# Where the value products of attention are issued: next to a round's scores, and a pair's second set one round earlier

## The chip, the cores and the metric

The kernel runs on one core of a Trainium2 chip. The metric is the device time of one execution in microseconds (us). PE is the matrix engine TensorE, PEld its weight loads, DVE is VectorE, ACT is ScalarE, POOL is GpSimd, and SP is the engine that issues the DMAs. Each engine executes the instructions of its own queue in the order in which the program issues them; between engines they wait for each other by semaphores.

## What is computed

Block-causal attention over 4 batches, 8 heads, 576 positions and head size 64; its output feeds a mixture of 8 experts (2304 tokens, width 512, hidden 1024) whose gate weights are normalised alternately over rows and columns eight times; that feeds a last two-layer network with a squared ReLU.

```python
scores = scale * np.matmul(q, k.transpose(0, 1, 3, 2))
mask = block_i >= block_j                      # blocks of 64 positions
attn = softmax(np.where(mask, scores, -1e9))
x = np.matmul(attn, v)                         # -> (2304, 512)
P = sinkhorn(exp(x @ w_gate), 8 rounds)        # (2304, 8)
for e in range(8):
    out += P[:, e:e + 1] * (np.maximum(x @ w1[e], 0) @ w2[e])
r = np.maximum(out @ w_in, 0); result = (r * r) @ w_out
```

## The kernel before

The 32 heads are worked off as 16 pairs (`PAIRS`). A pair has `R = 6` rounds of scores: the nine key-block widths are packed into six groups (`ROUNDS`), and `scores` issues the groups of an even round and of the next odd one together, so that only even rounds have scores. The whole attention is one software pipeline over rounds `r`, counted through all pairs: in round `r` the pair `r // 6` has its scores, and later steps of earlier rounds follow at fixed distances. Steps of round group i of a pair:

- scores on PE (`scores`, L563), into PSUM tiles sc and, in the pair's round 4, a small rest tile sct;
- one round later the maxima on DVE (`soft`, L582 to L593) and the exponentials on ACT (`expo`, L604);
- `LAG = 3` rounds after the scores the normalisation of pb by DVE (L620) or POOL (L616);
- four rounds after the scores the transposes on PE (`trans`, L643; the last group has a fifth, L646), five rounds after them their copies out of PSUM on ACT (`evac`, L657 and, for the fifth, L659), into ptx for the groups 0 to 2 and into pty for 3 to 5;
- the value products on PE (`pv`, L687), in two sets: the first reads ptx, the second pty. `PVT` holds the round, counted from the pair's start, in which each set is issued: 8 and 11;
- one round after a set (`PVD = 1`) ACT's copy of it into xs (`pv_copy`, L694), and after the second set the DMAs of xs to memory (`xout`, L699) and the pair's part of the gate logits (`logits_part`, lp on PE, L713, and its addition into prob on DVE, L724 or L726), the latter for pairs 4 and up.

Inside a round the steps are issued in the order of the table `ORDER`; "soft" is the maxima and normalisation, "pvc" the copy of a set with its DMAs, "load" the loads and `logits_part`, "hi" the `evac` copies, "exp" the exponentials, "S" the scores, "fill" the filling, "pv" the sets, "T" the transposes. The events of one engine therefore stand in its queue in this order, round after round.

The filling is the work of the experts. It is cut into pieces (a product m of a stage, L309 to L311, or an output tile y, L371 to L373), each costed at about one microsecond, and `fill` issues as many per round as the budget of 1.05 us allows. A product is followed by DVE's combination (L315), by ACT's ReLU where a hidden block is complete (L284), and by conversions of the next stage's weights (ACT L169 and L177, POOL L170, L178 and L153). Filling can only begin when the first third of the tokens has its gate logits (`logits`, lg on PE, L820) and its operands formed (`form`: sums f on POOL, L237; copies x on ACT, L243; rests x on DVE or POOL, L244). These two run as a task that is queued behind the DMAs of pair 7 (`first_ready`), two steps per round after a head start of three steps. So pairs 0 to 8 have no filling in their rounds, and the later ones have. In the attention part the products, outputs, transposes, sets, sct and lp share four PSUM buffers. After the attention the rest of the filling runs without it, to the end of the program.

```python
PVT = (8, 11)
PVD = 1
...
def turn(r):
    return [(n, z) for z, o in enumerate(PVT) for n in [(r - o) // R]
            if (r - o) % R == 0 and 0 <= n < PAIRS]
...
for r in range(total + R + LAG):
    for e in ORDER:
        events[e](r)
```

Of the kernel before, what the change touches and what calls it, by code (L numbers as in the profile page):

```python
# [55 lines left out]

POFF = {7: 0, 3: 2496, 6: 512, 5: 2752, 8: 1024, 0: 1600, 2: 1728, 4: 1984, 1: 2368}

ORDER = ["soft", "pvc", "load", "hi", "exp", "S", "fill", "pv", "T"]

POOL_NORM = (1, 4, 6, 8)

# [1 line left out]

LAG = 3

PVT = (8, 11)

PVD = 1

# [29 lines left out]
def fused_kernel(ctx: ExitStack, tc: tile.TileContext, q, k, v, wg, w1, w2, u1, u2, ident, out):  # L100
# [401 lines left out]
    def attention():  # L502
        with ExitStack() as es:
# [267 lines left out]
# [3 lines that stand above are left out]
# [35 lines left out]
# [3 lines that stand above are left out]
# [130 lines left out]
```

## Time and profile before

| what | before |
|---|---|
| median of 3 runs | 2097.63 us (2095.95 to 2098.12) |
| span of the profiled execution, first to last instruction | 2094.2 us |
| PE busy | 2064.7 us (99%) |
| DVE busy | 1653.6 us (79%) |
| POOL busy | 1566.2 us (75%) |
| ACT busy | 922.2 us (44%) |
| mean granted TensorE clock | 0.997 of full speed |

The profiled execution is one execution recorded by the hardware profiler; its device time without the recording isn't given beside it, so its span is set against the runs: the median lies 3.4 us above the span. A matmul counts as busy from its start to a modelled end, and neighbours overlap, so the busy share of PE isn't how near it is to its peak; the chain of waits and the starts of instructions say more. In a row of the chain, the time of a piece is the time that the chain spent in it. In a row of a timeline, the bracket at the end says how long the engine was idle before the instruction and what released it. The shape behind a matmul's names begins with the part of the array that it uses (contraction rows by output rows): 64\*64 for scores, 128\*64 for the sets, 128\*128 for transposes and filling.

### The profile page before, as it was taken

What the parts mean: (1) busy time and instruction counts of PE and PEld (TensorE: products, weight loads), DVE (VectorE), ACT (ScalarE), POOL (GpSimd) and SP (SyncE); (2) the same over time, 40 slices, a digit from 0 to 9 for tenths busy, and PEclk for the clock granted to TensorE, in tenths of its full rate; (3) what the DMA queues carried; (4) which work ended last, traced back from release to release, by engine and by line L of the source; (5) the groups of instructions that cost most, each with busy time, mean ns of one, the idle gap of its engine ahead of it and who ended that gap; (6) DMA issues with size and microseconds to landing.
All of it is one profiled execution on the core that took longest, in us unless ns stands there. A gap on an engine that the chain in (4) does not pass through costs nothing.

```text
span 2094.2 us, 34229 instructions
## 1 busy us (share of the span) xinstructions
PE 2064.7 (99%) x11603; PEld 1828.2 (87%) x11603; DVE 1653.6 (79%) x2906; ACT 922.2 (44%) x2299; POOL 1566.2 (75%) x1767
## 2 busy tenths in 40 slices
PE   8989999999999999999999999999999999999999
PEld 5767888999999899999999989999999989989898
DVE  7777678878878677878888768778787668989987
ACT  7876443334433533334434343333434344444442
POOL 4374566788887677778898777777897767989974
PEclk9999999999999999999999999999999999999999
DMA  5524111322222322232322233233222123231311
GB/s 177 153 89 130 52 64 68 117 90 93 94 79 94 120 77 87 100 106 86 101 78 91 94 106 98 89 106 109 78 76 86 61 81 103 69 131 61 103 69 51
DMA packets 80718, 194.71 MB, mean 93 GB/s; under 512 B 26144, under 2 KB 27296, under 8 KB 80544
## 3 DMA queue, kind: packets, MB, share of 16 engines
q1 hardware_dynamic: 80544, 192.53, 27.7%
q8 instruction: 92, 1.51, 0.3%
q14 instruction: 82, 0.67, 0.1%
HBM read 169.95 MB, written 20.97 MB: 91 GB/s over the span
## 4 chain that ended last, share of the span: by engine, by line
PE 90%; DVE 7%; ACT 1%; issue 1%; POOL 1%; DMA 0%; SPq 0%; ACTq 0%; DVEq 0%; POOLq 0%
PE y L371 15%; PE y L372 15%; PE y L373 15%; PE m L309 13%; PE m L311 13%; PE m L310 13%; PE T L643 2%; PE pv L687 2%; PE sc L563 2%; DVE c L289 2%; DVE acc L384 1%; DVE c L315 1%; DVE h L291 1%; DVE h L285 1%; ACT h L290 1%
## 5 line engine op out<-in xcount | busy, mean ns | idle before, releaser
L371 PE MATMUL y<-b,h 128*128 128x512 f32 x1440 | 564.4, 392 | 6.3 <-DVE acc L384 4.6
L309 PE MATMUL m<-x,ah 128*128 128x384 f32 x1680 | 566.7, 337 | 0.5 <-ACT m L320 0.4
L373 PE MATMUL y<-b,h 128*128 128x512 f32 x1440 | 565.7, 393 | 0.0
L372 PE MATMUL y<-b,h 128*128 128x512 f32 x1440 | 565.0, 392 | 0.0
L311 PE MATMUL m<-x,al 128*128 128x384 f32 x1680 | 564.4, 336 | 0.0
L310 PE MATMUL m<-x,ah 128*128 128x384 f32 x1680 | 563.1, 335 | 0.5 <-POOL x L244 0.5
L170 POOL TENSOR_TENSOR al<-sum,ah 128x256 fp32r<-128x256 f32 x480 | 402.2, 849 | 149.7 <-ACT ah L169 138.6
L391 DVE SCALAR_TENSOR_TENSOR acc<-y,prob,acc 128x512 f32<-128x512 f32 x516 | 375.0, 744 | 114.0 <-PE y L373 112.0
L178 POOL TENSOR_TENSOR b<-raww,b 128x512 fp32r<-128x512 f32 x240 | 319.0, 1329 | 180.8 <-ACT b L177 180.7
L284 ACT ACTIVATE h<-c 128x384 fp32r<-128x384 f32 x384 | 202.0, 526 | 563.1 <-DVE c L315 561.6
L170 POOL TENSOR_TENSOR al<-raww,ah 128x256 fp32r<-128x256 f32 x360 | 285.4, 793 | 78.8 <-ACT ah L169 71.0
L309 PEld LDWEIGHTS m<-x,ah 128*128 128x128 f32 x1680 | 315.5, 188 | 13.6 <-issue 1.4
L371 PEld LDWEIGHTS y<-b,h 128*128 128x128 f32 x1440 | 270.9, 188 | 61.4 <-DVE acc L384 2.8
L310 PEld LDWEIGHTS m<-x,ah 128*128 128x128 f32 x1680 | 315.5, 188 | 10.1 <-POOL x L244 0.8
L285 DVE SCALAR_TENSOR_TENSOR h<-c,h 128x384 fp32r<-128x384 f32 x384 | 315.9, 834 | 6.9 <-ACT h L284 5.1
L373 PEld LDWEIGHTS y<-b,h 128*128 128x128 f32 x1440 | 270.5, 188 | 57.4
L311 PEld LDWEIGHTS m<-x,al 128*128 128x128 f32 x1680 | 315.2, 188 | 0.0
L372 PEld LDWEIGHTS y<-b,h 128*128 128x128 f32 x1440 | 270.6, 188 | 50.7
L169 ACT ACTIVATE ah<-sum 128x256 fp32r<-128x256 f32 x480 | 183.4, 406 | 87.3 <-POOL sum L153 84.4
L153 POOL TENSOR_TENSOR sum<-raww 128x256 f32<-128x256 f32 x240 | 193.8, 807 | 0.0
L315 DVE TENSOR_TENSOR c<-m,u 128x384 f32<-128x384 f32 x240 | 132.0, 550 | 47.4 <-PE m L311 47.2
L320 ACT ACTIVATE m<-m 128x384 f32<-128x384 f32 x120 | 58.8, 490 | 228.5 <-PE m L311 228.1
(97 smaller groups left out, 2327.6 us busy)
## 6 DMA issues: line engine op xcount, KB each, us to landing
raww<-w_t SPq DMA_DIRECT2D x192, 512.0 KB, 3.5
raww<-w1f SPq DMA_DIRECT2D x24, 512.0 KB, 3.2
raww<-w2f SPq DMA_DIRECT2D x24, 512.0 KB, 3.2
q<-q_d SPq DMA_DIRECT2D x15, 576.0 KB, 4.6
raw<-w_in_bits SPq DMA_DIRECT2D x16, 512.0 KB, 4.7
raw<-w_out_bits SPq DMA_DIRECT2D x16, 512.0 KB, 4.7
acc<-xd SPq DMA_DIRECT2D x30, 256.0 KB, 4.3
v<-v_p SPq DMA_DIRECT2D x16, 320.0 KB, 5.6
```

Source lines behind the costliest of these rows:

```text
L153: nc.gpsimd.tensor_tensor(out=t[:, o], in0=x, in1=y, op=op)
L170: nc.gpsimd.tensor_tensor(out=lo, in0=src, in1=hi.bitcast(F32), op=ALU.subtract)
L178: nc.gpsimd.tensor_tensor(out=lo[:, f], in0=src, in1=hi[:, f].bitcast(F32), op=ALU.subtract)
L284: nc.scalar.activation(out=hh, in_=x3, func=ACTF.Relu)
L285: wait.append(lambda: nc.vector.scalar_tensor_tensor(out=hl, in0=x3, scalar=0.0, in1=hh.bitcast(F32), op0=ALU.max, op1=ALU.subtract,))
L309: nc.tensor.matmul(p, ah[:, k2], bh[:, k2], start=(k2 == 0), stop=False)
L310: nc.tensor.matmul(p, ah[:, k2], bl[:, k2], start=False, stop=False)
L311: nc.tensor.matmul(p, al[:, k2], bh[:, k2], start=False, stop=(k2 == 1))
L371: nc.tensor.matmul(p, hh, bh[:, f], start=(f == 0), stop=False)
L372: nc.tensor.matmul(p, hh, bl[:, f], start=False, stop=False)
L373: nc.tensor.matmul(p, hl, bh[:, f], start=False, stop=(f == 1))
L391: nc.vector.scalar_tensor_tensor(out=a, in0=p, scalar=pe, in1=a, op0=ALU.mult, op1=ALU.add)
```

## The change

Two constants are changed. In `ORDER` the sets stand ahead of the filling of their round, directly behind the scores, and the second set of a pair is issued in its round 10 in place of 11.

```diff
-ORDER = ["soft", "pvc", "load", "hi", "exp", "S", "fill", "pv", "T"]
+ORDER = ["soft", "pvc", "load", "hi", "exp", "S", "pv", "fill", "T"]
...
-PVT = (8, 11)
+PVT = (8, 10)
```

PE in the part without filling, at the end of pair 1 (pv with pty is the second set; T are the transposes of the next pair; sc and sct scores):

```order
@@ -49,5 +48,4 @@
 L563 MATMUL sc_111<-k,q 64x512 x2
 L563 MATMUL sct<-k,q 64x64 x2
-L643 MATMUL T<-idn,pb 128x128 x4
 L687 MATMUL pv<-pty,v 64x2x64 x2
 L687 MATMUL pv<-pty,v 64x64 x2
@@ -58,5 +56,5 @@
 L687 MATMUL pv<-pty,v 64x2x64 x2
 L687 MATMUL pv<-pty,v 64x64 x4
-L643 MATMUL T<-idn,pb 128x128 x4
+L643 MATMUL T<-idn,pb 128x128 x8
 L563 MATMUL sc_112<-k,q 64x128 x2
```

Four transposes that stood between the scores and the second set now stand behind the set, beside the four that were there.

ACT at the same place (L659 is the copy of a pair's fifth last transpose, L604 exponentials, L694 the copy of the second set, L657 copies of the next pair's transposes):

```order
 L659 ACTIVATE pty<-T_331 64x128
 L604 ACTIVATE pb,sm<-sc_111,nm 128x448
+L694 ACTIVATE xs<-pv 128x192
 L657 ACTIVATE ptx<-T 128x4x128
 L604 ACTIVATE pb,sm<-sc_112,nm 128x512
-L694 ACTIVATE xs<-pv 128x192
 L657 ACTIVATE ptx<-T 128x2x256
```

The copy of the set moved ahead of one copy of transposes and one exponential.

PE in the part with filling, a round with scores and a first set, before (y is an output tile of the filling):

```order
L563 MATMUL sc_112<-k,q 64x320 x2
L371 MATMUL y<-b_2074,h_2059 128x512
L372 MATMUL y<-b_2075,h_2059 128x512
L373 MATMUL y<-b_2074,h_2060 128x512
L371 MATMUL y<-b_2074,h_2061 128x512
L372 MATMUL y<-b_2075,h_2061 128x512
L373 MATMUL y<-b_2074,h_2062 128x512
L687 MATMUL pv<-ptx,v 64x128 x12
L643 MATMUL T<-idn,pb 128x128 x4
```

and the same round with the change (m is a product of the filling):

```order
L563 MATMUL sc_112<-k,q 64x320 x2
L687 MATMUL pv<-ptx,v 64x128 x12
L309 MATMUL m<-x_75,ah 128x384
L310 MATMUL m<-x_76,ah 128x384
L311 MATMUL m<-x_75,al 128x384
L309 MATMUL m<-x_75,ah 128x384
L310 MATMUL m<-x_76,ah 128x384
L311 MATMUL m<-x_75,al 128x384
L643 MATMUL T<-idn,pb 128x128 x4
```

The set stands behind the scores and the filling between the set and the transposes; that the piece of filling is another one comes from the filling's start, which is a round earlier.

## Rows read from the trace of the kernel before

**Rows 1.** The page, busy us of each engine, share of the span, instructions.

```profile
PE 2064.7 (99%) x11603; PEld 1828.2 (87%) x11603; DVE 1653.6 (79%) x2906; ACT 922.2 (44%) x2299; POOL 1566.2 (75%) x1767
```

**Rows 2.** Table by stretches: us, PE, PEld, DVE, ACT, POOL busy, PE clock, DMA.

```profile
60.00:70.00 10.00, 9.96 (x133) 7.37 (x131) 7.90 (x35) 8.77 (x29) 3.07 (x5) 1.00 0.64 186
...
120.00:130.00 10.00, 6.55 (x37) 4.30 (x35) 8.27 (x16) 7.62 (x25) 8.36 (x9) 0.83 0.20 66
```

**Rows 3.** Chain of waits, pair 4's round 10 to 12: start us, us, what.

```profile
62.05 1.02 PE sc L563 x8
63.06 0.11 PE sct L563 x4
63.18 0.59 PE T L643 x4
...
63.80 1.68 PE pv L687 x36
65.48 0.59 PE T L643 x4
66.06 0.57 PE lp L713 x6
```

**Rows 4.** Timeline of ACT, first half: start us, us, line, out<-in, shapes, [idle before].

```profile
41.96 0.49 ACT L694 ACTIVATE xs<-pv 128x384 f32<-128x384 f32 x1 [1.80 <-PE pv L687]
...
58.97 0.37 ACT L604 ACTIVATE pb<-sc,nm 128x128 f32<-128x128 f32 x1 [0.23 <-DVE sm L623]
...
63.12 0.63 ACT L657 ACTIVATE pty<-T 128x512 f32<-128x512 f32 x1
63.60 0.27 ACT L659 ACTIVATE pty<-T 64x128 f32<-64x128 f32 x1
...
64.37 0.60 ACT L657 ACTIVATE ptx<-T 128x512 f32<-128x512 f32 x1
...
65.53 0.33 ACT L694 ACTIVATE xs<-pv 128x192 f32<-128x192 f32 x1
66.10 0.60 ACT L657 ACTIVATE ptx<-T 128x512 f32<-128x512 f32 x1 [0.24 <-PE T L643]
```

**Rows 5.** Chain of waits, first half (first row) and with filling.

```profile
59.45 1.46 PE pv L687 x24
...
160.44 1.46 PE pv L687 x24
...
165.22 0.43 PE y L371
...
166.12 0.23 PE y L371
...
166.80 0.44 PE T L643 x4
...
169.92 0.59 PE T L643 x4
```

**Rows 6.** Timelines of PE (first row) and ACT behind a product of the filling.

```profile
167.97 0.34 PE L311 MATMUL m<-x,al 128*128 128x384 f32 x1
...
168.94 0.53 ACT L284 ACTIVATE h<-c 128x384 fp32r<-128x384 f32 x1 [0.35 <-DVE c L315]
169.37 0.40 ACT L169 ACTIVATE ah<-sum 128x256 fp32r<-128x256 f32 x1
```

**Rows 7.** Timelines of PE and ACT, the last transpose of pair 15 and its copy.

```profile
230.86 0.27 PE L646 MATMUL T<-idn,pb 128*64 128x128 f32 x1
...
232.01 0.26 ACT L659 ACTIVATE pty<-T 64x128 f32<-64x128 f32 x1
```

**Rows 8.** Chain of waits between the logits of the first third.

```profile
100.30 0.49 PE T L643 x4
100.79 0.91 PE sc L563 x9
```

**Rows 9.** Timeline of PE, pair 9's last transposes.

```profile
123.79 1.11 PE L643 MATMUL T<-idn,pb 128*128 128x128 f32 x4 [3.44 <-POOL pb L616]
```

## The prediction

> **What bounds the kernel now.** Three views were read in this order. The page's busy times say that PE is the bound: 2064.7 of 2094.2 us [rows 1], so what counts is where PE waits, what it pays between kinds of matmul, and what the change does to both. The table by stretches splits the attention part (the first 235 us) in three. In its first half (to about 105 us, no filling yet) ACT is nearly as full as PE, 8.77 of 10 us [rows 2]. Then comes a crowded stretch, 105 to 140 us, in which the first token group's operands are formed: POOL is busy 8.36 of 10 us, PE down to 6.55 [rows 2]. After it PE runs through with filling between the attention's rounds. The chain of waits and the timelines then give the prices at the places where the value products (the "sets": L687, 24 records for a pair's first set, 36 for its second) stand.
>
> **First half: the second set.** Before, PE runs in a pair's round 10 the scores (1.02 + 0.11 us), then four transposes of the next pair (0.59), and the second set at 63.80 [rows 3]. The set reads what ACT copies out of the pair's last transposes; the second of these copies (L659) begins at 63.60 and lasts 0.27 [rows 4], so the set starts when ACT allows it, and the four transposes fill PE's time until then. Moved to round 10, the set stands straight behind the scores. The copy doesn't come earlier: ACT has no idle time between its exponential at 58.97, which waits for DVE's maxima of new scores, and 66.10 [rows 4]. So the set still starts near 63.80, PE stands idle for about the 0.6 us before it, and the transposes come after the set, where they lie on PE's path to the next scores: one more group of four at 0.44 us, the price of four transposes without a change of array shape [rows 5]. Eight pairs (0 to 7) lie in this half: 8 x 0.44 = **+3.5 us**. Lower end 1.8, if ACT gains half of that slip where it now waits for PE (0.24 at 66.10); the upper end, 7.5, is the second rival's.
>
> With the set move ACT's copy of it (L694, 192 columns), SP's output DMAs behind that copy, the small logits products (lp, 0.57 us for three [rows 3]) and DVE's addition of them, from round 12 to 11. On SP the DMAs pass at most a weight load or two; no wait for a load stands in the chain of this half, so they cost nothing. PE had four transposes between set and lp and has four after, so lp waits no longer than now. DVE's addition gets ahead of the maxima of the pair's last scores and holds them until lp is done; ACT's exponential of them is not yet due, since ACT is late itself (second rival).
>
> **Second half: fewer changes of shape.** The first filling matmul behind scores takes 0.43 us in the chain where its like takes 0.23, and the four transposes behind a set take 0.59 where they take 0.44 behind filling [rows 5]. A set costs 1.46 us alike, behind scores at 59.45 and behind filling at 160.44 [rows 5]. Before, a round with scores and a set pays 0.20 (scores to filling) and 0.15 (set to transposes); after, only 0.20 (set to filling). Six pairs (9 to 14 for the second set, 10 to 15 for the first) have both kinds with filling: 12 x 0.15 = **-1.8 us**. Ends: 0, and 12 x 0.35 = -4.2 if the step from scores to set were free as well. The Trainium skill, TensorEngine Tiling, Key Properties, says that a change of tiling mode drains TensorE; scores (64x64) to sets (128x64) is such a change, so by it three changes per set stay of four, and one of mean price 0.175 is saved, -2.1 instead of -1.8. The trace agrees as far as it shows it: the two returns cost 0.20 and 0.15.
>
> Against this stands the lp of pairs 9 to 11: its last product is a half block of 64 rows, which before was followed by scores and is now followed by filling. One more return at 0.20, three times: **+0.6 us**.
>
> **Second half: new waits.** Here each wait of PE is a loss, since nothing else covers it. Filling used to stand between the copies on ACT and the products that need them. The row of a hidden block shows the delay that filling itself puts on ACT: its product's last matmul starts at 167.97, ACT's relu for it only at 168.94, the weight copy behind it at 169.37 and for 0.40 [rows 6]. So ACT is free about 1.5 us after PE has issued such a product (0.18 behind that last start, at 168.15).
> - The second set. By the order after, ACT's two copies of the last transposes stand behind such a relu for pairs 10, 12 (with a second weight copy) and 14. The two take 0.75 (63.12 to 63.87 [rows 4]), so they end 2.25 us behind the product; PE needs 0.55 for five transposes and 1.13 for the scores. Waits: 0.5, 0.8, 0.5, rounded down since a start can overlap the end before it. Pair 15 has no scores in round 10; before, its copy ended at 232.27 where the last transpose starts at 230.86 [rows 7], and PE filled the time. Wait: 1.3.
> - The logits. lp needs the set's copy, which now comes behind the filling of round 10 on ACT. Pair 11 (a relu and a weight copy before it): ready after 1.5 + 0.33 (65.53 [rows 4]), PE has 0.44 of transposes and 0.57 of lp's first three products, which read the first set only: 0.7. Pair 10 (an evacuation and a weight copy, without DVE's step ahead): 0.4.
>
> Sum 4.2; lower end 0 (ACT gains time where it no longer waits for the sets), upper end 6. I take **+4.0**.
>
> **The crowded stretch.** A pair's output is issued a round earlier, and so the tasks that start behind pair 7's: logits of the first group, then the forming of its operands. In PE's order the last logits no longer stand behind one group of four transposes (0.49) and one of scores (0.91) [rows 8], so forming can start 1.4 us earlier. POOL is more than eight tenths full there [rows 2], so somewhat over half of this should reach the end: **-0.8 us**. Ends: -3.4, if the wait of 3.44 us at 123.79 for POOL's scaling [rows 9] vanishes; +1.0, if POOL's new order delays that scaling.
>
> **Sum.** +3.5 - 1.8 + 0.6 + 4.0 - 0.8 = +5.5 us. The profiled span is 2094.2; the runs (median 2097.63) lie 3.4 above it, and nothing in that edge changes. 2094.2 + 5.5 + 3.4 gives **2103.1 us**, 0.26% slower.
>
> **Rivals.**
> - *No slower: POOL's gap closes and ACT keeps up.* Mechanism: forming starts a round earlier, POOL reaches the scaling that the last transposes wait for before PE gets there (the 3.44 us at 123.79 vanish), and in the second half ACT, which no longer stands waiting for sets, has its copies ready. Then 3.5 - 1.8 + 0.6 - 3.4 = -1.1: 2096.5 us. It decides from the point where POOL finishes that scaling as PE ends the transposes before. For it: POOL has time before that, 3.07 us busy of 10 in the first half [rows 2]. Against: by the order after, two more forming operations stand ahead of that scaling. Chance 0.20.
> - *Slower still: ACT becomes the first half's bound.* The copy of the second set now stands on ACT ahead of the next transposes' copy and an exponential. It can't start before the set ends, near 65.48 [rows 3], while ACT comes to that place at 64.37 [rows 4]: 1.1 us idle per pair. ACT is busy 8.77 of 10 us [rows 2], so 9.9 of every 10 would be taken, and the waits that stay (for DVE's maxima, for the next transposes) would lengthen the pair, by 0.5 us if two such waits of 0.23 to 0.24 remain [rows 4]: 8 x 0.5 = +4 more, 2107.1 us. The trace shows the like: at 41.96 ACT stood 1.80 us for a set [rows 4]. The Trainium skill, TensorE: Matmul & The Clock Gate, Architectural detail, calls ScalarE a strict FIFO, so that what stands behind the copy waits too; by that rule this rival is the stronger. It decides from the point where ACT comes to the next pair's first exponential later than DVE has the maxima for it; the pair's 0.44 us of growth give ACT some of the time back. Chance 0.22.
> - *The step from scores to sets is free.* Then -4.2 instead of -1.8: 2100.7 us. Against it stands the equal 1.46 us [rows 5]. Chance 0.08.
>
> **Chances and range.** My forecast has 0.50, and its own spread of a few us (2099 to 2106) crosses +0.2%, about what a measurement of this kernel can tell from no change (2101.8): 0.33 of it above, 0.17 within. The rival that is no slower gives 0.13 within and 0.07 below 2093.4 (its terms at their lower ends), the second 0.22 above, the third 0.08 within. Together: slower 0.55, same 0.38, faster 0.07. The range reaches from the first rival to beyond the second: 2096.5 to 2108.5.
>
> **What would show it.** Right: in the first half a PE wait for ACT's L659 ahead of the 36-record set, eight transposes behind it, and pairs 0.4 to 0.5 us longer; in the second half waits of 0.4 to 1.4 us at L687 and L713, and transposes at 0.44 behind filling. Wrong: a first half as long as before, or by 1 us per pair longer; no wait at the sets of pairs 10, 12, 14 and 15; a crowded stretch that is shorter or longer by over 2 us.

## The result, and the profile after

The changed kernel takes 2112.88 us (median of 5 runs, 2111.29 to 2114.39), the kernel before 2096.92 in the same job: ratio 1.0074, 95% interval [1.0063, 1.0085], so 16.0 us or 0.74% slower. The forecast was 2103.1 us, its range ended at 2108.5: the sign was right, the size was not. The profiled execution has a span of 2109.1 us against 2094.2.

The page's busy times say nothing of it. Set beside [rows 1], PE's work is the same to 1.4 us, and so is every other engine's to 3.3:

```profile
PE 2066.1 (98%) x11603; PEld 1830.3 (87%) x11603; DVE 1656.9 (79%) x2906; ACT 921.7 (44%) x2299; POOL 1564.9 (74%) x1767
```

The table by stretches shows where the time went (columns as in [rows 2]: length, busy us of PE, PEld, DVE, ACT and POOL, then PE's granted clock). First the kernel before:

```profile
0.00:320.00 320.00, 303.35 (x2779) 240.04 (x2780) 230.88 (x722) 209.66 (x620) 166.50 (x207) 0.99 0.35 110
...
30.00:40.00 10.00, 8.12 (x102) 5.25 (x96) 9.15 (x33) 9.98 (x35) 9.12 (x13) 0.92 0.54 167
40.00:50.00 10.00, 10.00 (x123) 7.17 (x123) 7.02 (x28) 7.50 (x25) 2.86 (x5) 0.91 0.48 155
...
127.00:250.00 123.00, 120.69 (x1104) 97.83 (x1099) 85.16 (x256) 78.21 (x226) 62.74 (x76) 1.00 0.30 91
```

and the changed kernel:

```profile
0.00:320.00 320.00, 290.81 (x2709) 229.46 (x2710) 221.38 (x694) 203.88 (x607) 158.16 (x198) 0.98 0.34 107
...
30.00:40.00 10.00, 7.18 (x98) 4.75 (x99) 9.05 (x31) 9.38 (x32) 8.40 (x13) 1.00 0.64 205
...
60.00:70.00 10.00, 9.35 (x127) 6.96 (x123) 7.35 (x34) 8.48 (x28) 2.80 (x4) 1.00 0.55 165
...
100.00:110.00 10.00, 10.00 (x80) 8.39 (x78) 3.56 (x13) 5.41 (x19) 3.80 (x4) 0.76 0.39 123
110.00:120.00 10.00, 8.88 (x111) 7.10 (x107) 7.83 (x22) 7.39 (x21) 7.76 (x9) 0.90 0.17 38
120.00:130.00 10.00, 6.65 (x64) 4.87 (x60) 8.39 (x20) 7.68 (x23) 8.71 (x9) 1.00 0.44 167
...
127.00:250.00 123.00, 110.52 (x1044) 88.32 (x1042) 81.23 (x247) 78.57 (x231) 63.88 (x76) 0.99 0.28 84
...
150.00:160.00 10.00, 7.68 (x69) 6.13 (x68) 8.72 (x20) 5.51 (x18) 6.73 (x8) 0.83 0.10 39
```

In the first 320 us PE is idle for 320 - 303.35 = 16.65 us before and 29.19 after: 12.5 us of the 14.9. Ten of them lie between 127 and 250 us (2.31 to 12.48). The rest is clock. Summed over stretches of 10 us, (1 - granted clock) x 10 gives 3.4 us before (0.92 and 0.91 at 30 to 50 us, 0.83 in [rows 2]) and 5.1 after (0.76, 0.90, 0.83). 12.5 + 1.7 = 14.2, and PE's idle time beyond 320 us adds 0.95 (12.86 to 13.81).

PE's waits by what ended them (us in total, times, longest) name the wait. Between 127 and 250 us of the changed kernel:

```profile
PE pv L687 <- ACT pty L657: 7.2, 5, 2.2
PE T L643 <- POOL pb L616: 2.1, 2, 1.8
PE pv L687 <- ACT ptx L657: 1.1, 1, 1.1
...
PE lp L713 <- ACT acc L380: 0.5, 2, 0.3
```

The kernel before has no wait at L687 there at all; its largest is 1.1 us at a transpose. Ahead of 100 us the changed kernel has 3.9 us in 8 waits at L687, before 0.2.

### The profile page after: what moved, and what is told of

Read it like the earlier page. It is cut to its first block, busy times and chain, and to the rows that moved or that the text cites. A ratio compares the mean times of both kernels' runs of the same rounds, so it can differ in the third digit from the quotient of the medians.

```text
span 2109.1 us, 34241 instructions
## 1 busy us (share of the span) xinstructions
PE 2066.1 (98%) x11603; PEld 1830.3 (87%) x11603; DVE 1656.9 (79%) x2906; ACT 921.7 (44%) x2299; POOL 1564.9 (74%) x1767
## 4 chain that ended last, share of the span: by engine, by line
PE 90%; DVE 6%; ACT 3%; issue 1%; POOL 0%; DMA 0%; SPq 0%; ACTq 0%; DVEq 0%; POOLq 0%
PE y L371 15%; PE y L372 15%; PE y L373 15%; PE m L309 13%; PE m L311 13%; PE m L310 13%; PE pv L687 2%; PE T L643 1%; ACT pb L604 1%; PE sc L563 1%; DVE c L289 1%; DVE c L315 1%; DVE acc L384 1%; DVE h L285 1%; DVE h L291 1%
```

## The experiments

Times are medians, with the ratio to the kernel before in the same job. For each kernel the table below sets the profiled span beside PE's idle time up to 320 us (320 minus PE's busy time there) and the time lost to the clock there (worked out as above). The last two columns are differences to before.

| kernel | idle | clock | idle + clock, more | span, more |
|---|---|---|---|---|
| before | 16.7 | 3.4 | | (2094.2) |
| the change | 29.2 | 5.1 | +14.2 | +14.9 |
| e1_order | 17.3 | 8.5 | +5.8 | +5.8 |
| e2_round | 21.3 | 3.4 | +4.6 | +4.8 |
| e3_no_fill9 | 32.2 | 8.5 | +20.6 | +22.0 |
| e4_tasks_early | 17.1 | 6.8 | +3.8 | +4.9 |
| e5_first_half | 21.5 | 5.1 | +6.5 | +5.8 |
| e6_second_half | 24.8 | 15.4 | +20.2 | +22.1 |
| e7_no_wait | 21.6 | 3.4 | +5.0 | +5.4 |
| e8_norm_dve | 26.6 | 6.8 | +13.3 | +12.2 |
| e9_copies_first | 38.2 | 11.9 | +30.0 | +31.7 |
| e10_first_set | 18.1 | 3.4 | +1.4 | +1.8 |

Two quantities account for every span within 2 us. An effect of the change that is smaller than that (of changes of array shape, of DMA queues) could still hide in what is left, -1.1 to +2.0 us. Each profile is of one execution, and executions of one kernel differ in the clock: e6 took 2112.65 to 2118.06 us, with the profile at the upper end, and e4 2096.5 to 2104.0 at a mean granted clock of 0.997 to 0.994.

**The two parts alone.** e1 keeps the new order of a round and puts the second set back to round 11:

```
-PVT = (8, 10)
+PVT = (8, 11)
```

> The new order of steps (sets ahead of the filling of their round), with the second set left in round 11. Theory A (the loss comes from the second set in round 10, which waits on PE for ACT's copies of the pair's last transposes, because these stand behind the ReLU of round 9's filling): those copies are a round old in round 11, so no waits at L687 with pty, and 2094 to 2100 us (six first sets save 0.15 each, lp waits for copies behind the filling of round 11 cost 0 to 3). Theory B (sets ahead of the filling lose by themselves): 2105 us or more. The first half is as before (second set of pair 7 at 94.2 us).

Measured: 2101.49 us, 1.0018 [1.0009, 1.0026], between the two ranges; no wait at L687 between 127 and 250 us, as theory A said. In the profiled execution 5.1 of the 5.8 us more are clock. e2 keeps round 10 and puts the filling back ahead of the sets:

```
-ORDER = ["soft", "pvc", "load", "hi", "exp", "S", "pv", "fill", "T"]
+ORDER = ["soft", "pvc", "load", "hi", "exp", "S", "fill", "pv", "T"]
```

> The second set in round 10, with the filling left ahead of the sets. Theory A: the first half as with the whole change (+1.6 us at pair 7's second set, 0.5 us per pair in steady state), in the second half a piece of filling of 1.05 to 1.4 us covers a part of the waits for L659, so L687 waits some 10 us less than the 9.6 us from 100 us on with the whole change where a piece of filling is there; 2098 to 2104 us. Theory C (round 10 is too early whatever stands ahead of the set): 2108 us or more, with waits of over 1 us at L687 left for pairs 9 to 15.

Measured: 2100.94 us, 1.0016 [1.0007, 1.0024]; waits at L687 between 127 and 250 us of 0.13 us; theory A held. The parts cost 3.7 and 3.1 us, both together 16.0: more than half of the loss is made by the pair of edits only. A second set can do without the round between its copies and itself if a piece of filling stands between (e2), and without the filling if it has the round (e1), but not without both.

**Is it the ReLU of the filling ahead of the copies?** e3 is the whole change without filling in a pair's round 9, whose budget goes to round 10:

```
-                budget[0] = min(budget[0] + FILL, 2.0)
-                if budget[0] > 0 and formed:
+                budget[0] = min(budget[0] + FILL, 3.0 if r % R == 4 else 2.0)
+                if budget[0] > 0 and formed and r % R != 3:
```

> The whole change, but a pair's round 9 issues no filling (its budget goes to round 10, behind the second set). Theory A: ACT then has no ReLU and no weight copy ahead of the copies of the last transposes; the waits at the second sets of pairs 9 to 15 (8.3 us from 127 us on) fall to below 3 us, and the time by 5 to 8 us to 2105 to 2108. Rival (ACT is late there through the attention's own exponentials and DVE's maxima): the waits stay at 6 us or more and the time within 2 us of 2112.9.

Measured: 2113.97 us, 1.0079 [1.0067, 1.0092]; waits for the copies at L687 stay at 6.1 us between 127 and 250 us. My first theory, that the ReLU alone delays the copies, fell, and its rival held. The timeline of ACT in e3 shows what still stands ahead of them at pair 11, an exponential that waits for DVE's maxima:

```profile
177.09 0.31 ACT L604 ACTIVATE pb<-sc,nm 128x64 f32<-128x64 f32 x1 [0.49 <-DVE nm L593]
...
177.90 0.59 ACT L657 ACTIVATE pty<-T 128x512 f32<-128x512 f32 x1
178.38 0.26 ACT L659 ACTIVATE pty<-T 64x128 f32<-64x128 f32 x1
```

PE had ended the last transpose at 176.51 and the scores at 177.64, and began the set at 178.54. Without filling PE also comes to the set sooner, so e3 takes away cover together with the ReLU and doesn't say how much each is worth.

**The earlier tasks alone.** e4 is the kernel before with its logits and forming tasks begun two task steps earlier (READY 3 to 1).

> The kernel before, with the tasks behind pair 7 (logits, forming of the operands) begun one round earlier (head start 1 in place of 3), sets untouched. With the whole change PE stood idle 2.9 us from 100 to 127 us in place of 5.4 and the first filling began 1.1 us earlier although the first half was 1.6 us later. If the earlier start made this, this kernel begins its filling 1.5 to 2.7 us earlier and takes 2094 to 2096 us. If it came from the sets' places, the filling begins at 126 to 128 us and the time is 2096 to 2098.

Measured: 2100.61 us, 1.0011 [1.0001, 1.0021]; a miss. Filling does begin at 124.0 in place of 127.2 us, and PE's idle time between 100 and 127 us falls from 5.36 to 2.38; but between 127 and 250 us it rises from 2.31 to 4.94, and the clock loses 3.4 us more (0.50 at 100 to 110 us). The idle time that an earlier start of the filling saves comes back behind it.

**Which half?** e5 and e6 give the second set's round by pair; e5 has before's order, e6 the new one (with the numbers swapped):

```
-                return [(n, z) for z, o in enumerate(PVT) for n in [(r - o) // R]
-                        if (r - o) % R == 0 and 0 <= n < PAIRS]
+                return [(n, z) for n in range(PAIRS) for z in range(2)
+                        if r - R * n == (8, 10 if n < 9 else 11)[z]]
```

> The second sets of pairs 0 to 8 stand in the pair's round 10, those of pairs 9 to 15 in round 11 as before; the order of a round is that of before (without filling, up to some 126 us, both orders are the same). Theory A (the first half costs 8 waits of some 0.5 us, of which the clock that no longer falls at 30 to 50 us gives most back, and the loss of the whole change lies in the second half): logits begin near 99.9 us, first filling 126 to 126.5, PE's idle time between 127 and 250 us under 4 us, 2098 to 2100.5. Rival B (the loss is set in the first half and the crowded stretch, where the logits lose clock, and runs on from there): 2103 to 2108, with the idle time between 127 and 250 us at 7 or more.

> The whole change from pair 9 on; the second sets of pairs 0 to 8 stand in round 11 as before. Theory A (the loss lies in the second half, where a second set right behind its scores finds the transposes' copies of ACT unfinished): 2106 to 2112, with 5 us or more of waits at the second sets between 127 and 250 us. Rival B (first half and crowded stretch): 2097 to 2102, with under 2 us of waits at the second sets.

Measured: e5 2103.45 us, 1.0033 [1.002, 1.0045]; e6 2117.2 us, 1.0089 [1.0075, 1.0103]. e6 has 5.8 us of waits at the sets between 127 and 250 us, as theory A said, and lies above A's range, since its clock lost 12 us more than before's; B, which gave it no loss, fell. e5 is a miss for A: its time lies at the lower end of B's range, and its 5.6 us idle between 127 and 250 us between A's under 4 and B's 7. Its longest waits there are:

```profile
PE T L643 <- POOL pb L616: 1.9, 2, 1.8
PE y L371 <- DVE c L315: 0.9, 1, 0.9
PE m L309 <- DVE acc L384: 0.8, 1, 0.8
```

All its nine waits there of 0.15 us or more are e4's, at the same instructions, some 4.2 us later and within 0.02 us as long. e4 has before's sets; what the two share is that logits and forming begin a round earlier. So this part of e5's loss comes from the earlier filling and not from the second sets themselves. The halves don't add up (7.1 + 20.9 against 16.0), so the time of one depends on how the other leaves the queues, and on the clock.

**Is it the wait?** e7 is the whole change, but from pair 9 on the second set reads the other transposed tile, so that it has none of ACT's last copies to wait for:

```
-                pt = pt_y if g else pt_x
+                pt = pt_y if g and n < 9 else pt_x
...
+            nc.gpsimd.memset(pt_x[:, 10:12], 0.0)
```

> The whole change, but from pair 9 on the second set reads the first set's transposed tile instead of its own, so it multiplies the wrong weights; all transposes and ACT's copies are still done, and the second set has nothing of ACT's last copies to wait for (the first set's tile gets a fill of two unused blocks at the start). Theory A (the loss is PE's wait for these copies): waits at the second sets between 127 and 250 us under 1.5 us, the time 2102 to 2106, near the sum of the two halves of the change alone (some 6.8 us over before). Rival C (ACT and DVE are behind by so much that the wait goes on to the next transposes, logits pieces or filling): second sets without waits, the idle time between 127 and 250 us still 9 us or more, 2109 to 2113.

Measured: 2104.1 us, 1.0037 [1.0024, 1.0049]: 7.8 us over before in place of the change's 16.0, with all instructions of ACT, DVE and POOL still there. No set waits any more for copies into `pty`. Of the 2.3 us of waits that remain at the sets (waits of PE, 127 to 250 us), 1.2 are at second sets, under A's 1.5; the 1.1 is at pair 15's first set:

```profile
PE pv L687 <- DVE c L315: 1.2, 2, 0.9
PE pv L687 <- ACT ptx L657: 1.1, 1, 1.1
PE m L309 <- DVE acc L384: 0.8, 1, 0.8
```

So the wait of the second sets for ACT's copies makes about half of the loss (8.2 of 16.0 us), and it does not simply move to the next instruction: theory A held, rival C fell. What is left is near the 6.8 us that the two parts cost alone.

**Why are the copies late?** In e8 DVE scales all weights of the attention and POOL none:

```
-POOL_NORM = (1, 4, 6, 8)
+POOL_NORM = ()
```

> The whole change with the scaling of blocks 1, 4, 6 and 8 on DVE in place of POOL: some 3.3 us of POOL a pair go, DVE gets an estimated 1.7 us a pair more (0.57 us for 512 elements in its own scalings). Theory D (ACT's copies are late because DVE's short operations last 0.8 to 1.2 us in place of 0.15 while POOL works, and these scalings are a good part of POOL's work): waits at the second sets between 127 and 250 us fall from 8.3 to under 5 us, 2105 to 2110; mean time of the short operations at L593 and L625 falls from 0.44 and 0.42 us to under 0.3. Rival E (DVE's queue is simply full, the added scalings make it later): waits as long or longer, 2113 to 2120.

Measured: 2108.39 us, 1.0059 [1.0046, 1.0071]: 12.1 us over before in place of 16.0, although DVE got the work; the time is in theory D's range. In the groups of DVE's instructions between 127 and 250 us the short ones become shorter; the changed kernel, then e8 (busy us, mean ns):

```profile
L625 DVE TENSOR_SCALAR sm<-sm 128x2 f32<-128x2 f32 (+1 forms) x30 | 9.2, 308 | 0.0
L593 DVE TENSOR_SCALAR nm<-mx 128x2 f32<-128x2 f32 (+1 forms) x28 | 8.9, 319 | 0.4
```

```profile
L625 DVE TENSOR_SCALAR sm<-sm 128x2 f32<-128x2 f32 (+1 forms) x30 | 7.5, 248 | 0.0
L593 DVE TENSOR_SCALAR nm<-mx 128x2 f32<-128x2 f32 (+1 forms) x28 | 6.6, 235 | 0.0
```

The waits at the sets fall only from 8.3 to 6.7 us, where theory D wanted under 5; of PE's idle time 2.6 us go, more than half of that ahead of 127 us (13.6 in place of 15.1). So POOL's load on DVE has a part in the lateness, 1.6 us of waits, and most of it has another source; rival E fell. In e9 the transposes stand ahead of the filling and ACT's copies right behind them; the second set stands in round 10 from pair 9 on:

```
-ORDER = ["soft", "pvc", "load", "hi", "exp", "S", "pv", "fill", "T"]
+ORDER = ["soft", "pvc", "load", "exp", "S", "pv", "T", "hi", "fill"]
...
-                "hi": lambda r: at_step(lambda _, j: evac(j), r - LAG - 2),
+                "hi": lambda r: at_step(lambda _, j: evac(j), r - LAG - 1),
```

> From pair 9 on both sets stand next to a round's scores, the second in the pair's round 10, as in the whole change; for pairs 0 to 8 the second set stands in round 11. In every round the transposes stand ahead of the filling, and ACT's copies of them are issued right behind them, ahead of the filling's work for ACT and a piece of filling earlier than in the whole change. Theory A (the loss is PE's wait for these copies, and an hour of ACT's queue between transposes and set decides it): waits at the second sets between 127 and 250 us under 2 us, PE's idle time there under 6 us, 2095 to 2101 us by how often the clock falls (1.7 us for each fall of some 3.4 us to half speed, as the earlier runs show). Rival F (the copies are late whatever their place, since exponentials and maxima stand ahead of them, and transposes ahead of the filling wait for their scaled weights): idle time there 8 us or more, 2104 to 2115.

Measured: 2128.21 us, 1.0143 [1.0129, 1.0157], outside both ranges, on rival F's side. PE's waits between 127 and 250 us:

```profile
PE T L643 <- POOL pb L616: 11.3, 7, 4.7
PE lp L713 <- ACT xs L694: 5.5, 5, 1.4
PE pv L687 <- ACT pty L657: 1.4, 1, 1.4
```

The sets' waits are down to 1.4 us, but e9 doesn't show why: the copies stand earlier in ACT's queue, and a piece of filling now stands on PE between the last transposes and the second set. In exchange the transposes, without filling ahead of them, wait for POOL's scaled weights, and the logits pieces for the sets' copies. In all these runs the filling covers whichever step stands behind it.

**A version without the loss.** e10 puts only the first sets next to the scores; the second stay behind the filling in round 11:

```
-ORDER = ["soft", "pvc", "load", "hi", "exp", "S", "fill", "pv", "T"]
+ORDER = ["soft", "pvc", "load", "hi", "exp", "S", "pv0", "fill", "pv1", "T"]
```

> Of the whole change only the first sets' place: next to the scores, ahead of the filling; the second sets stand behind the filling in the pair's round 11 as before. Theory A (the first sets have their copies in time and the second sets keep their cover): no waits at the sets between 127 and 250 us, PE's idle time up to 320 us within 1.5 us of before's 16.7, 2095 to 2098 with as many falls of the clock as before, 1.7 us more for each further one. Rival G (the order next to scores costs by itself, as where both sets stood there in round 11): 2099 to 2103 without more falls of the clock.

Measured: 2098.32 us, 1.0004 [0.9995, 1.0013]: no difference from before. As theory A said, no set waits between 127 and 250 us and PE's idle time up to 320 us is 1.4 us over before's; the time lies between A's 2098 and rival G's 2099. No run beat the kernel before.

## Why the prediction was wrong in size

**The term that failed: "second half: new waits", +4.0; it measured 9.3.** The mechanism was right, and so was the place: sets without filling ahead of them wait for ACT. The 4.0, rounded from 4.2, held 3.1 for four sets (pairs 10, 12, 14, 15: 0.5, 0.8, 0.5, 1.3) and 1.1 for two logits pieces. Measured at the sets (timeline of PE, the rows with a wait):

```profile
134.50 1.68 PE L687 MATMUL pv<-pty,v 128*64 128x128 f32 x36 [1.61 <-ACT pty L657]
155.76 2.47 PE L687 MATMUL pv<-pty,v 128*64 128x128 f32 x36 [2.24 <-ACT pty L657]
...
192.99 1.68 PE L687 MATMUL pv<-pty,v 128*64 128x128 f32 x36 [0.69 <-ACT pty L657]
...
229.84 1.68 PE L687 MATMUL pv<-pty,v 128*64 128x128 f32 x36 [1.15 <-ACT pty L657]
239.66 1.53 PE L687 MATMUL pv<-ptx,v 128*64 128x128 f32 x24 [1.12 <-ACT ptx L657]
246.01 1.68 PE L687 MATMUL pv<-pty,v 128*64 128x128 f32 x36 [1.52 <-ACT pty L657]
```

These are pairs 9, 10, 12, 14, 15 (first set) and 15: 8.3 us. The second sets of pairs 12 and 15 came out at 0.7 and 1.5, about as priced; pair 10 cost 2.24 and pair 14 1.15 in place of 0.5 each, and pair 9 and pair 15's first set, 2.7 together, were not on the list. The logits' waits were 0.95 against 1.1. All of PE's idle time in this stretch grew by 10.2 us.

The price came from one row of the kernel before: a ReLU that begins 0.97 us behind its product's last start [rows 6]. After the change that delay is 1.0 us ahead of the second sets of pairs 12 and 15, but 1.8 at pair 14 and 3.2 at pair 10. For pair 10 after the change that product's last matmul starts at 151.22 and the ReLU (`h<-c`) at 154.39, 3.17 us later. ACT's timeline shows why, and DVE's and POOL's behind it:

```profile
153.05 0.31 ACT L604 ACTIVATE pb<-sc,nm 128x64 f32<-128x64 f32 x1 [0.54 <-DVE nm L593]
...
154.39 0.52 ACT L284 ACTIVATE h<-c 128x384 fp32r<-128x384 f32 x1 [0.42 <-DVE c L315]
154.82 0.40 ACT L169 ACTIVATE ah<-raww 128x256 fp32r<-128x256 f32 x1
155.13 0.58 ACT L657 ACTIVATE pty<-T 128x512 f32<-128x512 f32 x1
155.60 0.26 ACT L659 ACTIVATE pty<-T 64x128 f32<-64x128 f32 x1
```

```profile
150.13 1.11 DVE L625 TENSOR_SCALAR sm<-sm 128x2 f32<-128x2 f32 x1
...
151.93 1.09 DVE L593 TENSOR_SCALAR nm<-mx 128x2 f32<-128x2 f32 x1
152.93 0.96 DVE L620 TENSOR_SCALAR pb<-pb,rc 128x384 f32<-128x384 f32 x1
153.81 0.54 DVE L315 TENSOR_TENSOR c<-m,m 128x384 f32<-128x384 f32 x1
```

```profile
149.68 1.53 POOL L616 TENSOR_TENSOR pb<-pb,rc 128x576 f32<-128x576 f32 x1
151.73 1.27 POOL L178 TENSOR_TENSOR b<-raww,b 128x512 fp32r<-128x512 f32 x1 [0.51 <-ACT b L177]
```

DVE's own queue is late: an operation on two numbers a partition (L625, L593), which takes 0.15 us at other places, takes 1.1 when it meets a POOL instruction, and ends when that ends (151.24 and 151.21; 153.02 and 153.00). The product's combination (`c<-m,m`) stands behind them, the ReLU behind that, the copies behind the ReLU, and PE behind the copies. A delay on DVE that the kernel before hides under filling thus reaches PE through two in-order queues. I priced only the last link, from one place where the combination came soon. This chain is read off the trace of one pair, and POOL isn't in all of them: at pair 14 L625 and L593 take 0.16 and 0.17 us, and the copies are late behind two exponentials, which wait for DVE's maxima, and the ReLU. e8 bears out POOL's share in part; no run shows the whole chain.

**First half: +3.5, right.** PE waits 3.9 us in 8 second sets, and a pair takes 10.62 us in place of 10.13 (first sets at 81.03 and 70.41, before at 79.64 and 69.51), 0.49 more where 0.44 was the price. The chain of waits at pair 4 (start, us) answers to [rows 3]:

```profile
63.44 0.49 ACT pty L657
...
63.98 1.68 PE pv L687 x36
65.65 0.58 PE T L643 x4
66.24 0.57 PE lp L713 x6
66.81 0.49 PE T L643 x4
67.30 0.91 PE sc L563 x13
```

The set starts when ACT allows it, as before, the logits piece comes 2.26 us later in both, and one more group of transposes (0.49) stands ahead of the next scores. In the change the logits nevertheless begin only 1.6 us later (100.09 against 98.45), because the clock did not fall at 37 to 42 us in this execution. e5, whose first half has the same instructions and where the clock does fall there (0.93 and 0.90 at 30 to 50 us), has them at 102.13: 3.7 us later.

**Fewer changes of shape: -1.8, not seen in the total.** The pieces came as priced: the chain of the change has 0.43 us for filling behind a set (at 187.54) and 0.44 for the transposes behind it (at 189.13). In the total it would show as a span below what idle time and clock make it. The change, which has all 12, lies at +14.9 against +14.2 (15.2 with the idle time beyond 320 us); e1 and e10, which have the first sets' half, at +5.8 against +5.8 and +1.8 against +1.4; e2, which has none, at +4.8 against +4.6. But other rows miss by up to 2 us without it, so a gain of the size forecast isn't excluded either. The Trainium skill, TensorEngine Tiling, Key Properties, on which the estimate of a still larger saving rested, says that a change of mode drains TensorE; no run here shows a gain in the total from having fewer of them. The +0.6 for half blocks can't be told apart either.

**The crowded stretch: -0.8.** PE's idle time between 100 and 127 us falls by 2.4 (5.36 to 2.94; the wait of [rows 9] becomes 1.6), more than forecast. The clock takes most of it back: it costs 3.4 us at 100 to 120 us, where before lost 1.7 a little later [rows 2]. The forecast also took an earlier start of the filling for a gain that lasts; e4 and e5 show that waits behind it take it back.

**The rivals.** "ACT becomes the first half's bound" came near in number (2107.1), by a cause that didn't act: ACT does stand for the set (1.04 us at 65.70, where 1.1 was said), but a pair grows by 0.49, not by 1. The 1.80 us at 41.96 that spoke for it [rows 4] stand behind a set that ran at the lower clock. "No slower" failed since the waits at the sets outweigh what POOL's gap gives. What the range lacked was a term for clock: no case moved it, and in the profiled executions it moved the time by up to 12 us (e6).

**All terms together.** For the profiled execution, against the forecast: waits of the second half's sets and logits 9.3 us (4.0), idle time up to 100 us 4.4 (3.5), between 100 and 127 us -2.4 (-0.8), clock 1.7 (none), idle time elsewhere 2.2 (none), changes of shape not seen (-1.2): 15.2 us, where the span grew by 14.9 and the forecast by 5.5.

## What to carry to other kernels

Before work is moved out from between a producer and its consumer, find how late the producer can be, over all repetitions and through all queues that feed it: the slack that filling hides is not in any wait of the profile, and one undisturbed row can price it too low. Two edits that can use the same slack have to be priced together: here 3.7 and 3.1 us alone, 16.0 both. When accounting for a difference, set PE's idle time and its granted clock side by side by stretches; together they left at most 2 us unexplained in every run.

## What was not expected of the hardware

- The clock. The losses come in steps of about 1.7 us (3.4, 5.1, 6.8, 8.5 in the table). A first set takes 1.53 us at 2.4 GHz and 2.83 at 1.2 GHz (before at 39.08, the change at 109.17). In the change the clock falls at 105 us, while PE runs 32 logits products of 8 columns one behind the other (4.23 us; before the same 32 took 3.74 without a fall). At 37 us it fell in before, behind a wait of 1.84 us, and not in the change, behind one of 2.19. Whether a fall comes isn't decided by the length of the wait just ahead of it alone; what decides it stays open.
- DVE beside POOL. L593 and L625, 0.15 to 0.17 us alone, can take up to 1.2 us when a POOL instruction is running, and then end with it. The Trainium skill, SBUF — State Buffer, SBUF: two separate sides, says that the port pair that DVE and GpSimd share is locked for a whole instruction and that the other blocks. The trace agrees for these operations. The maxima (L582) show no such thing: the longest takes 0.69 us beside POOL and 0.69 without.
